# Cosine attention and a two-layer feed-forward on one core: from the third batch on, attention products in 64-row by 32-column tiles for two quads at once

## The chip, the cores and the metric

The kernel runs on one core of a Trainium2 chip. A core has a matrix engine (TensorE, "PE" in the profile, its weight loads "PEld"), a vector engine (VectorE, "DVE"), an activation engine (ScalarE, "ACT"), a general engine (GpSimd, "POOL") and a queue engine (SyncE, "SP"). The engines run their own instruction streams in order and wait for each other through semaphores. PE reads SBUF and writes PSUM, which has 8 banks of 128 partitions by 512 fp32; ACT and DVE read PSUM. The metric is the device time of one execution in microseconds; the median of three runs before the change is 428.21 us (426.97 to 428.27).

## The reference

Attention over 8 batches, 12 heads, 448 positions, 64 numbers per head, with queries and keys divided by their norms and the scores by tau = 0.1; then two matrix products with a leaky ReLU between:

```python
q_n = q / (norm(q) + 1e-06);  k_n = k / (norm(k) + 1e-06)
attn = softmax(q_n @ k_n.T / tau)          # per batch and head, 448 x 448
x = (attn @ v) as [8 * 448, 12 * 64]       # 3584 x 768
h = x @ w_in;  g = max(0.01 * h, h);  out = g @ w_out     # 768 -> 2048 -> 768
```

The scores are at most 10, so the kernel takes exp without subtracting the maximum.

## The kernel before, in words

A batch's 12 heads are 6 pairs, and 3 quads of two pairs (quad j has pairs 2j and 2j+1). A **slot** s is one pair of one batch, 0 to 47.

**Preparation of a slot.** Queries and keys are loaded (SP queue), squared on POOL (`squares`, L163), summed over each row on DVE (`sums`, L174), turned into norms by three small ACT instructions (`roots`, L181 to L183), inverted and multiplied in on DVE (`normalise`, L191 and L195), and transposed by a DMA on the SP queue (`transposes`, L227) into `qkT`, where PE reads them. `hold` (L426) is a one-element copy on POOL that makes POOL wait for the end of a slot's `normalise` before it squares the next slot.

**Attention.** A key tile is 128 keys of a pair's two heads against 448 queries: four products of 64 rows (one head's 64 numbers) by 64 columns (half of the keys), which write two PSUM banks (`key_tiles`, L251); ACT takes exp into a bf16 tile (L263). A quad has seven such tiles: three for each pair, and one that holds the last 64 keys of both pairs. `attend(j)` then makes three sets of products for the quad (L274): the sums of exp (weights are ones), and the values in two halves of the 64 numbers (e = 0, 1). Each set is 4 passes (3 main key tiles and the rest) of four 128-row by 32-column products, one head to a strip of 32 columns; in the pass for the rest, half of the 128 rows are weights of zero. ACT makes 1/sum by Ln and Exp (L285, L286) and DVE multiplies it into the values, writing `xT` (`scale`, L305).

**Feed-forward.** The 3584 rows are 8 chunks: of each two batches (896 rows) an even chunk of 384 rows that needs the first batch only, and an odd chunk of 512 that needs both. A chunk has 16 groups `first` (6 products of 128x128 by 384 or 512, then a leaky ReLU on ACT, L323 and L329) and 6 or 8 groups `second` (16 products by 384, then a copy of the result by DVE into `osb`, L359, and a store on the SP queue).

**Order.** There is no scheduler: instructions are issued in the order in which Python writes them. From the second batch on, attention goes in **units** (seven to a batch): in three of seven units an `attend`, then three key tiles, then `sums`, `roots` and `normalise` of a slot some units ahead with its transposes and loads, and then feed-forward groups of the batch before, as many as an even share allows. PSUM banks are dealt by `banks`, which takes the banks that were dealt longest ago. A unit with `attend` takes 9 banks (one for the sums, two for the values, six for the scores), one without takes six, before its feed-forward groups.

```python
            if at is not None:
                attend(b * NQ + at)
                load_v(b * NQ + at + 2)
            key_tiles([(b * NPAIR + p, ki) for p, ki in tiles])
            ...
            sums(s)
            roots(s)
            ...
                normalise(s)
            ...
            while len(queue) > 1 and (i == len(units) - 1 or done + queue[0][0] / 2 <= share):
                cost, fn = queue.pop(0)
                fn()
```

## Time and profile before

| | |
|---|---|
| Median of three runs | 428.21 us (426.97 to 428.27) |
| The profiled execution's own time | 427.37 us |
| Its span, first to last instruction | 425.6 us |
| PE busy | 414.2 us (97%) |
| ACT busy | 267.3 us (63%) |
| DVE busy | 187.8 us (44%) |
| POOL busy | 138.0 us (32%) |
| Mean granted PE clock | 0.998 |

The profile is of one execution. Busy time is the time in which at least one instruction of the engine is under way; PE's products are pipelined and overlap, so the start times in the timeline tell more of their pace than the durations. A line of the page or of the table of groups names the source line, the engine, the operation, what is written from what, the shape, the count, then busy time and mean duration. A line of the timeline gives a start, a duration and how many like instructions were merged.

### The profile page before, as it was taken

Reading aid. Unit: us, or ns where it says so; the run is one execution under the profiler, and the core shown is the slowest. Engines: PE = TensorE matmul, PEld = TensorE weight load, DVE = VectorE, ACT = ScalarE, POOL = GpSimd, SP = SyncE. Lnnn points to the kernel's source line nnn. Section 1 sums busy time; section 2 is a strip of 40 time slices with the busy share of each in tenths; the row PEclk is TensorE's granted clock in tenths of the full one; section 3 lists DMA queues with packets and bytes.
Section 4 is the critical chain, followed back from the end, with each engine's and each line's share of the span. In section 5 each row is a group of like instructions: output and inputs, shape, how many; then the busy total and the mean of one; then the engine's idle time right before and its main releaser. Section 6 shows DMA issues by size and latency. Waiting matters only on the chain.

```text
span 425.6 us, 9170 instructions
## 1 busy us (share of the span) xinstructions
PE 414.2 (97%) x3571; PEld 210.8 (50%) x3585; DVE 187.8 (44%) x367; ACT 267.3 (63%) x494; POOL 138.0 (32%) x208
## 2 busy tenths in 40 slices
PE   8789999999999999999999999999999999999995
PEld 3234555544555555544455555544455555554563
DVE  5886767443363445343453454553343541220021
ACT  3997886667644786577663786568745686434300
POOL 3876543523124233513224132621424110000000
PEclk9999999999999999999999999999999999999999
DMA  5999999965458555953758356864547322010022
GB/s 142 219 229 219 224 218 197 242 151 123 93 121 169 103 130 104 210 126 79 131 90 171 100 124 129 164 128 129 97 105 138 78 60 42 39 74 2 0 75 75
DMA packets 102890, 53.68 MB, mean 126 GB/s; under 512 B 68928, under 2 KB 97856, under 8 KB 102848
## 3 DMA queue, kind: packets, MB, share of 16 engines
q1 hardware_dynamic: 76880, 40.75, 40.0%
q0 software_dynamic: 25056, 11.80, 21.6%
q8 instruction: 28, 0.46, 0.5%
q10 hardware_dynamic: 912, 0.56, 0.4%
q14 instruction: 14, 0.11, 0.1%
HBM read 45.61 MB, written 11.01 MB: 133 GB/s over the span
## 4 chain that ended last, share of the span: by engine, by line
PE 82%; DMA 10%; ACT 4%; DVE 2%; issue 1%; POOL 1%; ACTq 0%; DVEq 0%; POOLq 0%; SPq 0%
PE ps L348 33%; PE ps L323 31%; PE ps L274 11%; PE ps L251 7%; DMA w_out_sb<-in_moe_w_out_dram 6%; DMA q_h<-in_q_dram 3%; ACT pe L263 2%; DVE qn L195 1%; DMA k_h<-in_k_dram 1%; POOL sq L163 0%; ACT pr L263 0%; ACT ss L183 0%; ACT ss L181 0%; ACT ss L182 0%; DVE ss L174 0%
## 5 line engine op out<-in xcount | busy, mean ns | idle before, releaser
L263 ACT ACTIVATE pe<-ps 128x896 bf16<-128x896 f32 x144 | 122.6, 918 | 47.9 <-PE ps L251 46.5
L348 PE MATMUL ps<-w_out_sb,hT 128*128 128x384 bf16 x896 | 152.0, 326 | 0.3 <-DMA w_out_sb<-in_moe_w_out_dram 0.3
L323 PE MATMUL ps<-xT,w_in_sb 128*128 128x384 bf16 (+1 forms) x757 | 150.2, 352 | 0.6
L348 PEld LDWEIGHTS <-hT 128*128 128x128 bf16 x896 | 85.2, 98 | 65.3 <-issue 10.0
L323 PEld LDWEIGHTS <-w_in_sb 128*128 128x128 bf16 x768 | 73.2, 98 | 73.1 <-issue 7.7
L329 ACT ACTIVATE hT<-ps 128x384 bf16<-128x384 f32 (+1 forms) x128 | 64.8, 540 | 41.1 <-PE ps L323 40.5
L426 POOL CAST seen<-qn 128x1 f32<-128x1 bf16 x47 | 8.6, 183 | 201.4 <-DVE qn L195 200.7
L359 DVE COPY osb<-ps 128x384 f32<-128x384 f32 (+1 forms) x56 | 30.9, 552 | 95.8 <-PE ps L348 89.4
L174 DVE TENSOR_REDUCE ss<-sq 128x6 f32<-128x384 f32 (+1 forms) x95 | 56.2, 612 | 19.8 <-POOL sq L163 18.2
L163 POOL TENSOR_TENSOR sq<-q_h 128x512 f32<-128x512 f32 x46 | 47.7, 1036 | 6.1 <-DMA q_h<-in_k_dram 5.0
L251 PE MATMUL ps<-qkT 64*64 64x448 bf16 (+1 forms) x636 | 44.7, 358 | 3.2 <-ACT pe L263 1.4
L191 DVE RECIPROCAL r<-ss 128x14 f32<-128x14 f32 x48 | 11.5, 241 | 78.5 <-ACT ss L183 78.5
L163 POOL TENSOR_TENSOR sq<-k_h 128x384 f32<-128x384 f32 x47 | 39.0, 830 | 6.0 <-DMA k_h<-in_k_dram 6.0
L305 DVE TENSOR_TENSOR xT<-ps,rb 128x448 bf16<-128x448 f32 x48 | 27.9, 619 | 29.6 <-ACT rb L286 28.1
L274 PE MATMUL ps<-pe,v_b 128*32 128x448 bf16 x576 | 35.6, 353 | 0.0
L195 DVE TENSOR_TENSOR qn<-q_h,r 128x512 bf16<-128x512 f32 x48 | 34.2, 713 | 2.2 <-DVE r L191 0.6
L285 ACT ACTIVATE rb<-ps 128x448 f32<-128x448 f32 x24 | 13.1, 544 | 32.8 <-PE ps L274 32.7
L251 PEld LDWEIGHTS <-qkT 64*64 64x64 bf16 (+1 forms) x636 | 14.8, 104 | 31.3 <-issue 23.8
L195 DVE TENSOR_TENSOR qn<-k_h,r 128x384 bf16<-128x384 f32 x48 | 27.1, 564 | 0.0
L263 ACT ACTIVATE pr<-ps 128x896 bf16<-128x896 f32 x24 | 22.2, 927 | 0.0
L274 PEld LDWEIGHTS <-v_b 128*32 128x32 bf16 x576 | 15.2, 97 | 11.9 <-issue 0.4
L150 POOL DMA_DIRECT2D v_rem<-in_v_dram x32 | 20.5, 646 | 0.0
(39 smaller groups left out, 183.1 us busy)
## 6 DMA issues: line engine op xcount, KB each, us to landing
q_h<-in_q_dram SPq DMA_DIRECT2D x48, 192.0 KB, 3.5
k_h<-in_k_dram SPq DMA_DIRECT2D x46, 192.0 KB, 3.7
out_dram<-osb SPq DMA_DIRECT2D x30, 192.0 KB, 3.1
v_b<-in_v_dram POOLq DMA_DIRECT2D x24, 192.0 KB, 5.2
out_dram<-osb SPq DMA_DIRECT2D x12, 384.0 KB, 3.1
w_in_sb<-in_moe_w_in_dram POOLq DMA_DIRECT2D x4, 768.0 KB, 10.5
w_out_sb<-in_moe_w_out_dram POOLq DMA_DIRECT2D x2, 1536.0 KB, 22.6
q_h<-in_q_dram SPq DMA_DIRECT2D x48, 32.0 KB, 3.7
```

The costliest lines, as they stand in the source:

```text
L150: gp.dma_start(out=vrb[b % 2][lo : lo + 64, :, g], in_=r[g])
L163: eng.tensor_tensor(sq, x, x, op=ALU.mult)
L174: nc.vector.tensor_reduce(o.rearrange("p (h t) -> p h t", h=2), sqs[s][i], axis=AX.X, op=ALU.add)
L195: nc.vector.tensor_tensor(qn[s][:, lo:hi], x.rearrange("p h t d -> p t h d"), r[:, r0 : r0 + 2 * nt].rearrange("p (h t) -> p t h", h=2) .u ...
L251: nc.tensor.matmul(out=sc[p : p + width, a, :S], lhsT=x[rows, c0 : c0 + width], rhs=x[rows, 0:S], start=True, stop=True,)
L263: nc.scalar.activation(out=dst, in_=sc[:, :, :S], func=AF.Exp, scale=inv_tau)
L274: nc.tensor.matmul(out=x[32 * g : 32 * g + 32, :S], lhsT=weights(g, ki) if ki < 3 else rem(g), rhs=pe[s][:, ki, a, :] if ki < 3 else pr[j] ...
L305: nc.vector.tensor_tensor(xT[m][:, 2 * jj + e, half * S : (half + 1) * S], pos.pop((j, e))[:, :S], rbs[j], op=ALU.mult,)
L323: nc.tensor.matmul(out=pm[:, :n], lhsT=w_in_sb[:, kt, m * 128 : (m + 1) * 128], rhs=xT[c // 2][:, kt, c0 : c0 + n], start=(kt == 0), stop= ...
L329: nc.scalar.activation(out=hT[c][:, m, :n], in_=pm[:, :n], func=AF.Prelu, alpha=0.01)
L348: nc.tensor.matmul(out=po2[:, :HALF], lhsT=hT[c][:, m, ts * 128 : (ts + 1) * 128], rhs=w_out_sb[:, m, half * HALF : (half + 1) * HALF], st ...
L359: nc.vector.tensor_copy(out=o[:, half * HALF : half * HALF + cut], in_=po2[:, :cut])
```

## The change

The first two batches (quads 0 to 5) stay as they are. For quads 6 to 23:

- **Key tiles.** A quad's seven tiles are each 64 keys of both of its pairs: eight products of 64 rows by 32 columns, four strips of 32 keys (two of one pair, two of the other) by two heads, into two banks as before (`quad_tiles`). All seven tiles are now full and alike. For this the keys are loaded in two halves (one more DMA per slot), and the values come as `vq`, in rows of 64 keys, by four DMAs per quad on POOL's queue (before: one per quad for the main keys and four per batch for the rest).
- **Sums and values.** They are made for a group of two quads at once (`group_products`): 7 passes of eight 64-row by 32-column products, into two banks, for the sums, for e = 0 and for e = 1. ACT's Ln and Exp become one pair of 128x896 per group; the multiplication into `xT` becomes four DVE instructions of 64 partitions by 448 per group and half. The last pass over zeros is gone.
- **Order.** The units become 42 **visits** of three tiles each, n = 0 to 41. A group's sums stand in the visit after its last tile, its two value halves in the two visits after that, each right behind that visit's three tiles. Then come `sums`, `roots`, `normalise`, the transposes and loads of one slot (visits 6, 13, 20, 27 and 34 have none, and there is none after visit 37), and then feed-forward groups. A chunk's groups are held back until the group with its last quad is done, and spread by a new rule. Three tiles and a set of products together take all 8 banks.
- **Pools.** One exp tile per key tile (27 buffers), 5 of `vq`, and one `hT` in place of two.

What the visits hold after their three tiles, in the order in which the program issues it:

| visit | products | feed-forward |
|---|---|---|
| 0 | | 1 second |
| 1 to 4 | | 4 first of 512, each |
| 5, 6, 7 | sums, e=0, e=1 | 1 second, each |
| 8, 9 | | 1 second, each |
| 10, 11, 12 | sums, e=0, e=1 | 1 second, each |
| 13 | | 8 first of 384 |
| 14 | sums | 8 first of 384 |
| 15, 16 | e=0, e=1 | 1 second, each |
| 17, 18 | | 2 second, each |
| 19, 20, 21 | sums, e=0, e=1 | 6, 4, 4 first of 512 |
| 22 | | 2 first, 1 second |
| 23 | | 2 second |
| 24, 25, 26 | sums, e=0, e=1 | 2, 1, 1 second |
| 27 | | 1 second, 3 first of 384 |
| 28, 29, 30 | sums, e=0, e=1 | 9 first, 4 first, 1 second |
| 31, 32 | | 2 second, each |
| 33 to 41 | sums 33, e=0 34, e=1 35; sums 38, e=0 39, e=1 40 | 31 groups in all |

After visit 41 come the last group's products and the rest of chunks 6 and 7.

```diff
-            engs[1].dma_start(out=k_h, in_=main(k, b, h0, 2))
+        if s < 2 * NEWQ:
+            engs[1].dma_start(out=k_h, in_=main(k, b, h0, 2))
+        else:
+            r = k[b, h0 : h0 + 2, 0:MAIN].rearrange("h (p u t) d -> u p h t d", u=2, t=3)
+            for u in range(2):
+                engs[1].dma_start(out=k_h[64 * u : 64 * u + 64], in_=r[u])
...
+    def quad_tiles(which):
+        tiles = []
+        for j, i in which:
+            sc = banks(2)
+            tiles.append(sc)
+            for strip in range(4):
+                x = qkT[2 * j + pair_in_half(j, strip // 2)]
+                c0 = 448 if i == 6 else 512 + 128 * (i % 3) + 64 * (i // 3)
+                c0 += 32 * (strip % 2)
+                for a in range(2):
+                    rows = slice(64 * a, 64 * a + 64)
+                    nc.tensor.matmul(
+                        out=sc[32 * strip : 32 * strip + 32, a, :S], lhsT=x[rows, c0 : c0 + 32],
+                        rhs=x[rows, 0:S], start=True, stop=True,
+                    )
+        for (j, i), sc in zip(which, tiles):
+            pq[j, i] = pe_tile()
+            nc.scalar.activation(out=pq[j, i], in_=sc[:, :, :S], func=AF.Exp, scale=inv_tau)
...
+    def group_products(g, e):
+        j0 = NEWQ + 2 * g
+        po = banks(2)
+        for i in range(7):
+            for strip in range(4):
+                for w in range(2):
...
+                    nc.tensor.matmul(
+                        out=po[32 * strip : 32 * strip + 32, w, :S],
+                        lhsT=weights, rhs=pq[j, i][rows, a, :],
+                        start=(i == 0), stop=(i == 6),
+                    )
+        if e is None:
+            rb = rbp.tile([128, 2, S], F32, name="rb")
+            nc.scalar.activation(rb, po[:, :, :S], func=AF.Ln)
+            nc.scalar.activation(rb, rb, func=AF.Exp, scale=-1.0)
...
+                nc.vector.tensor_tensor(
+                    xT[m][rows, 2 * jj + e, half * S : (half + 1) * S],
+                    po[rows, w, :S], grb[g][rows, w], op=ALU.mult,
+                )
...
+    for n, tiles in enumerate(visits):
+        if n == 0:
+            attend(NEWQ - 1)
+        quad_tiles(tiles)
+        if n in parts:
+            group_products(*parts[n])
...
+        s = b * NPAIR + 3 + u if u < 6 else NSLOT
+        sums(s)
+        roots(s)
+        if s < NSLOT:
+            normalise(s)
+            transposes(s)
+            load_qk(s + 4)
+            hold(qn[s][:, 6, 0, 0:1])
+            squares(s + 1)
+        for j, i in tiles:
+            if i == 0:
+                load_vq(j + 1)
+        done = 0
+        while held:
...
+            fn()
```

## The prediction

> **What bounds the kernel now.** First the page's busy shares and its slices, then the table by stretch:

> ```profile
> PE 414.2 (97%) x3571; PEld 210.8 (50%) x3585; DVE 187.8 (44%) x367; ACT 267.3 (63%) x494; POOL 138.0 (32%) x208
> PE   8789999999999999999999999999999999999995
> 105.00:387.00 282.00, 281.58 (x2492) 145.81 (x2497) 118.35 (x228) 180.51 (x330) 82.54 (x124) 1.00 0.54 112
> ```

> From 105 to 387 us PE is busy for 281.58 of 282 us at a granted clock of 1.00: nothing makes it wait. So each pass taken from PE is worth its price, and each wait put in costs its length. The timeline of PE gives the price of a pass:

> ```profile
> 200.87 0.75 PE L274 MATMUL ps<-pe,ones 128*32 128x448 bf16 x12
> 201.44 0.36 PE L274 MATMUL ps<-pr,ones_rem 128*32 128x448 bf16 x4
> 201.63 0.74 PE L274 MATMUL ps<-pe,v_b 128*32 128x448 bf16 x12
> ...
> 202.96 0.36 PE L274 MATMUL ps<-pr,v_rem 128*32 128x448 bf16 x4
> 203.25 0.76 PE L251 MATMUL ps<-qkT 64*64 64x448 bf16 x12
> 203.94 5.35 PE L323 MATMUL ps<-xT,w_in_sb 128*128 128x512 bf16 x23
> ```

> From 200.87 to 201.63 are 4 passes: 0.19 us each, four products at once. The last pass starts at 202.96, the next shape at 203.25 and not at 203.15: a change of tile shape costs 0.10. Three key tiles take 203.94 - 203.25 - 0.10 = 0.59, so 0.19 each.

> Then the timeline of all engines, where a slot is prepared as fast as it can be:

> ```profile
> 61.14 0.55 DVE L195 TENSOR_TENSOR qn<-k_h,r 128x384 bf16<-128x384 f32 x1
> 61.83 0.18 POOL L426 CAST seen<-qn 128x1 f32<-128x1 bf16 x1 [4.54 <-DVE qn L195]
> 62.03 1.03 POOL L163 TENSOR_TENSOR sq<-q_h 128x512 f32<-128x512 f32 x1
> 63.03 0.82 POOL L163 TENSOR_TENSOR sq<-k_h 128x384 f32<-128x384 f32 x1
> 63.09 1.34 DVE L174 TENSOR_REDUCE ss<-sq 128x8 f32<-128x512 f32 x2 [1.41 <-POOL sq L163]
> 64.47 0.31 ACT L181 ACTIVATE ss<-ss,tiny 128x14 f32<-128x14 f32 x1 [0.69 <-DVE ss L174]
> 65.05 0.31 ACT L183 ACTIVATE ss<-ss,eps 128x14 f32<-128x14 f32 x1
> 65.39 0.24 DVE L191 RECIPROCAL r<-ss 128x14 f32<-128x14 f32 x1
> 66.27 0.55 DVE L195 TENSOR_TENSOR qn<-k_h,r 128x384 bf16<-128x384 f32 x1
> ```

> One slot's `normalise` ends at 61.69, the next one's at 66.82. Every link waits for the one before: `hold` for `normalise`, squares for `hold`, sums for squares, `roots` for sums, `normalise` for `roots`. So 5.14 us is the shortest step from slot to slot, whatever PE does. A unit before lasts 8.2 us here (203.25 to the next tiles at 211.83), so that never showed. Last, where a copy of the feed-forward stands in DVE's order:

> ```profile
> 163.47 2.77 PE L348 MATMUL ps<-w_out_sb,hT 128*128 128x384 bf16 x16
> ...
> 167.44 0.55 DVE L195 TENSOR_TENSOR qn<-k_h,r 128x384 bf16<-128x384 f32 x1
> 167.91 0.55 DVE L359 COPY osb<-ps 128x384 f32<-128x384 f32 x1
> ```

> The group ends near 166.2, its copy starts at 167.91, behind the unit's `normalise`. Nobody needed the bank yet.

> **The change part by part.** The sum is made against the profiled execution's 427.37 us, 0.84 under the median.

> *Passes.* Key tiles stay at 126 for 18 quads. Sums and values fall from 18 x 12 = 216 to 9 x 21 = 189: 27 x 0.19 = 5.1 us less. The price of a pass of eight is shown nowhere. Bounds: 0.19, since row halves (the 64x64 tiles) and column strips (128x32) each already run side by side at 0.19; and 0.38, if the halves took turns. I take 0.19: the rows show both ways of splitting. [...]

> *Shape changes.* Scores and products now have one shape. Before: 42 units x 2, 18 more for the attends, 2 at the end: 104. After: 84 + 1 + 4 = 89. 15 x 0.10 = 1.5 us less. PE gains 6.6 in all.

> *Waits in short visits.* A second group is 16 x 0.1625 = 2.6 us (from 5.31 us between shape changes for 32 products, in the chain). A visit with one is 0.57 + 0.20 + 2.6 = 3.4 us of PE, with products (7 x 0.19) 4.7. Both are under 5.14, and in a visit with products all 8 banks are taken again, so the product pair takes the bank of the visit before's second group, whose copy stands behind `normalise`. Prices: exp 0.85 each from 0.43 after the tile's start (203.25 to 203.69); the three roots 0.87; sums 1.14; reciprocal and two products 1.41; copy 0.55; hand-over 0.06. The xT scaling is 4 x 0.58 = 2.3 (1.16 for two in the trace; a 64-partition form is not shown: between half, if all elements counted, and the same, as 448 per partition are unchanged; I take the same). Ln and Exp of 128x896: 544 and 576 ns at half the width; I take 0.85 and 0.95, as exp of 128x896 does.

> Visit 5 (sums): exps, Ln and Exp, roots, `normalise` end 7.46 us after its start, the copy 8.07. Visit 6's products could start at 4.86 + 0.67 = 5.53: **wait 2.54**. From visit 7's start as zero: products leave at 2.4, scaling 4.7, sums 5.85, roots 6.8, `normalise` of slot 21 at 8.2. Then:
> - Visit 9 opens quad 10, which needs slot 21 transposed: 8.2 + 2.95 (landing, the DMA part's 2.9, and hand-over) = 11.2; PE is there at 8.5: **2.75**.
> - Slots 22 and 23: 8.2 + 2 x 5.14 = 18.5. Copy 19.1. Visit 10's sums need its bank; PE is there at 15.0: **4.15**.
> - Slot 24, behind these sums and their Ln and Exp: 24.9 (6.3 later). Visit 11's products wait for the copy at 25.5; PE at 23.9: **1.62**.
> - Now a step is copy 0.61, products 1.57, scaling 2.3, sums 1.14, roots 0.99, `normalise` 1.41 = 8.0: slot 25 at 32.9. Visit 12: **3.34**. Slot 26 at 40.9, copy 41.5; visit 13's second first-group takes that bank: **2.27**.

> These make 16.7. The same order (an e = 0 visit with one second group, then e = 1) gives 3.34 at visits 16 and 26 each; visits 17 and 18, 31 and 32 with two second groups wait 0.64 + 1.77 each time for the copies of the visit before; visit 27 0.64, visit 30 1.86: 14.0 more. Visits 1 to 4, 14, 19 to 24, 28, 29 and 33 to 37 hold about 6 us of PE or more, visits 38 to 41 prepare nothing: some twenty waits under 0.6, 3.4 together, which I leave to the range. Sum 30.7.

> *Beside it.* ACT: 9 x 1.8 in place of 18 x 1.12, less in all, but in one lump ahead of `roots` (counted). POOL: 72 issues for values at 0.65 to 0.80 in place of 18 + 24: in a quad's first visit squares (2.2) and four issues (up to 3.2) make 5.4 against a step of 5.14, so up to 0.3 in the stretch of visits 7 to 9, in the range. SP: one more key DMA, 0.4 us: transposes 1.26, five loads 2.5 to 3, under 5.14. One `hT`: a chunk's last second group ends on PE before the next chunk's first, no price.

> 427.4 - 6.6 + 30.7 = 451.5, on the median's side **452 us**. [...]

> **The rivals.**
> - *Slack is lent (faster).* 33 preparations stand in some 260 us of PE: 8 us each against steps of 5 to 8, so short visits could live on what long ones leave. It speaks for it that slots are prepared two to three visits ahead, and that PE waits for almost nothing now. Against it: a bank can't be lent, as the next visit takes it. It decides where all waits stay under 6.6 us; with none, 428.2 - 6.6 = 421.6.
> - *Waits only where a bank is forced.* Visits 6, 12, 16, 26 and part of 10, without what they hand on: 10 to 17 us, 432 to 438.
> - *The clock drops in the waits.* Granted 1.00 throughout, but no PE wait over 1.5 us stands in this trace. If each of the four waits of 3.3 us and more halved the clock for as long again, 4 x 1.7 = 7 us: 459. [...]
> - *Row halves take turns.* 315 x 0.19 = 60 us more: 487 without waits, 512 with them.

> **How the numbers follow.** Waits as worked out, with or without the clock (440 to 464): 0.61. Forced waits only (428 to 440): 0.17. Slack lent (419 to 426.9): 0.17. No difference beyond 0.3%, 1.3 us, about what a measurement can tell (426.9 to 429.5): 0.03. Over 464: 0.02. The range 428 to 464 leaves out the faster cases and the top: 0.8 inside. Faster 0.17, same 0.03, slower 0.80.

> **What would show it.** Right: PE waits on DVE's osb copy at the product line's first products in visits 6, 10, 11, 12, 16 and 26, 2 to 4 us each; on qkT's transposes once, in visit 9; DVE's sums wait on POOL's squares in step; passes of eight at 0.19. Wrong: PE still 97% busy, or passes at 0.38, or `normalise` well under 5 us after the last one's, or copies issued before it.

## The result and the profile after

The changed kernel takes 460.07 us (median of six runs, 458.07 to 461.37), the kernel before beside it 428.03 us: 1.075 times as long, with a 95% interval of 1.0719 to 1.0781. Forecast were 452 us, 428 to 464. The profiled execution took 461.37 us, 34.0 more than the profiled one of before; the sum of the prediction had 24.1.

The busy time of PE, its slices and the granted clock, from the page of the changed kernel:

```profile
PE 423.1 (92%) x4720; PEld 216.9 (47%) x4737; DVE 214.2 (47%) x403; ACT 265.7 (58%) x476; POOL 152.7 (33%) x238
PE   8789999999878699699999879998999999999996
PEclk9999999999897989989999989999999999999999
```

PE was a full row of nines. Now the slices from the eleventh on have holes, and the clock has them nearly where PE has. The table by stretch, from the same start to 34 us later than 387, as the profiled execution is 34 us longer:

```profile
105.00:421.00 316.00, 291.64 (x3618) 152.71 (x3613) 142.25 (x259) 177.10 (x309) 93.45 (x147) 0.97 0.48 99
```

PE is idle for 24.4 of 316 us, where it was idle for 0.4 of 282, and its clock is 0.97. What PE waited for (line waited for: us in all, times, longest), in the view of waits:

```profile
PE ps L378 <- DVE osb L449: 15.5, 6, 3.5
PE ps L438 <- DVE osb L449: 3.5, 3, 1.6
PE ps L355 <- DMA qkT<-qn: 2.5, 1, 2.5
```

L378 is the products of `group_products`, L438 the `second` groups, L355 the tiles of `quad_tiles`, L449 the copy of a `second` group out of its bank. The timeline shows one such wait, in visit 6 (lines of PE and DVE; those of the other engines are left out):

```profile
115.35 0.76 PE L355 MATMUL ps<-qkT 64*32 64x448 bf16 x24
...
116.19 0.24 DVE L216 RECIPROCAL r<-ss 128x14 f32<-128x14 f32 x1 [3.60 <-ACT ss L208]
116.47 0.69 DVE L220 TENSOR_TENSOR qn<-q_h,r 128x512 bf16<-128x512 f32 x1
117.07 0.55 DVE L220 TENSOR_TENSOR qn<-k_h,r 128x384 bf16<-128x384 f32 x1
117.54 0.55 DVE L449 COPY osb<-ps 128x384 f32<-128x384 f32 x1
...
118.15 1.67 PE L378 MATMUL ps<-pe,vq 64*32 64x448 bf16 x56 [2.04 <-DVE osb L449]
...
119.75 4.25 PE L438 MATMUL ps<-w_out_sb,hT 128*128 128x384 bf16 x16
```

The group whose bank is copied had ended by 115.35. DVE sat idle for 3.60 us until `roots` (L208) came, then did `normalise` first and the copy after it. The first products waited 2.04 us for that bank. The `second` group behind them, 2.77 us elsewhere, took 4.25: the granted clock was 0.50 from 119.38 to 122.79 (shown under the hardware below). This is called the half clock from here on.

The step from slot to slot, on DVE, a few visits later:

```profile
137.00 0.55 DVE L220 TENSOR_TENSOR qn<-k_h,r 128x384 bf16<-128x384 f32 x1
137.47 0.55 DVE L449 COPY osb<-ps 128x384 f32<-128x384 f32 x1
138.96 1.34 DVE L199 TENSOR_REDUCE ss<-sq 128x8 f32<-128x512 f32 x2 [0.94 <-POOL sq L188]
141.26 0.24 DVE L216 RECIPROCAL r<-ss 128x14 f32<-128x14 f32 x1 [0.96 <-ACT ss L208]
...
142.15 0.55 DVE L220 TENSOR_TENSOR qn<-k_h,r 128x384 bf16<-128x384 f32 x1
```

From one `normalise` to the next are 5.15 us (forecast 5.14), and between them DVE waits for POOL's squares and then for ACT's roots. The price of a pass of eight can be read in visit 8, in PE's timeline:

```profile
128.88 0.76 PE L355 MATMUL ps<-qkT 64*32 64x448 bf16 x24
129.57 2.77 PE L438 MATMUL ps<-w_out_sb,hT 128*128 128x384 bf16 x16
```

Three tiles and a change of shape take 129.57 - 128.88 = 0.69 us: 0.19 or 0.20 a pass, when 0.10 is taken off for the change.

### The profile page after: what moved, and what is told of

It is laid out like the page before. It is cut to its first block, busy times and chain, and to the rows that moved or that the text cites. A ratio compares the mean times of both kernels' runs of the same rounds, so it can differ in the third digit from the quotient of the medians.

```text
span 459.5 us, 11553 instructions
## 1 busy us (share of the span) xinstructions
PE 423.1 (92%) x4720; PEld 216.9 (47%) x4737; DVE 214.2 (47%) x403; ACT 265.7 (58%) x476; POOL 152.7 (33%) x238
## 4 chain that ended last, share of the span: by engine, by line
PE 60%; DMA 14%; DVE 12%; ACT 6%; issue 4%; SPq 1%; POOL 1%; DVEq 0%; POOLq 0%
PE ps L413 25%; PE ps L438 22%; PE ps L378 9%; DMA w_out_sb<-in_moe_w_out_dram 5%; DVE xT L397 5%; DMA q_h<-in_q_dram 4%; PE ps L355 4%; DMA q_h<-in_k_dram 3%; DVE ss L199 3%; DVE qn L220 3%; DVE osb L449 1%; ACT ss L208 1%; POOL sq L188 1%; ACT ss L206 1%; ACT pe L361 1%
## 5 line engine op out<-in xcount | busy, mean ns | idle before, releaser
L438 PE MATMUL ps<-w_out_sb,hT 128*128 128x384 bf16 x896 | 158.4, 335 | 4.8 <-DVE osb L449 3.5
L361 ACT ACTIVATE pe<-ps 128x896 bf16<-128x896 f32 x126 | 106.3, 921 | 32.1 <-PE ps L355 31.9
L438 PEld LDWEIGHTS <-hT 128*128 128x128 bf16 x896 | 87.4, 100 | 76.3 <-issue 22.6
L397 DVE TENSOR_TENSOR xT<-ps,rb 64x448 bf16<-64x448 f32 x72 | 44.8, 622 | 64.1 <-PE ps L378 63.3
L449 DVE COPY osb<-ps 128x384 f32<-128x384 f32 (+1 forms) x56 | 30.7, 552 | 69.8 <-PE ps L438 69.2
L206 ACT ACTIVATE ss<-ss,tiny 128x14 f32<-128x14 f32 x48 | 14.8, 309 | 56.0 <-DVE ss L199 55.4
L378 PE MATMUL ps<-pe,vq 64*32 64x448 bf16 x1008 | 30.3, 368 | 13.4 <-DVE osb L449 13.3
L288 ACT ACTIVATE pe<-ps 128x896 bf16<-128x896 f32 x42 | 35.8, 916 | 5.9 <-PE ps L279 4.5
L355 PE MATMUL ps<-qkT 64*32 64x448 bf16 x1008 | 33.4, 353 | 3.2 <-DMA qkT<-qn 2.5
L378 PEld LDWEIGHTS <-vq 64*32 64x32 bf16 x1008 | 16.5, 95 | 24.8 <-issue 15.4
L169 POOL DMA_DIRECT2D vq<-in_v_dram x36 | 23.0, 638 | 0.5 <-issue 0.3
L173 POOL DMA_DIRECT2D vq<-in_v_dram x36 | 22.5, 624 | 0.0
```

The source lines that it names most:

```text
L288: nc.scalar.activation(out=dst, in_=sc[:, :, :S], func=AF.Exp, scale=inv_tau)
L355: nc.tensor.matmul(out=sc[32 * strip : 32 * strip + 32, a, :S], lhsT=x[rows, c0 : c0 + 32], rhs=x[rows, 0:S], start=True, stop=True,)
L361: nc.scalar.activation(out=pq[j, i], in_=sc[:, :, :S], func=AF.Exp, scale=inv_tau)
L378: nc.tensor.matmul(out=po[32 * strip : 32 * strip + 32, w, :S], lhsT=weights, rhs=pq[j, i][rows, a, :], start=(i == 0), stop=(i == 6),)
L397: nc.vector.tensor_tensor(xT[m][rows, 2 * jj + e, half * S : (half + 1) * S], po[rows, w, :S], grb[g][rows, w], op=ALU.mult,)
L438: nc.tensor.matmul(out=po2[:, :HALF], lhsT=hT[c][:, m, ts * 128 : (ts + 1) * 128], rhs=w_out_sb[:, m, half * HALF : (half + 1) * HALF], st ...
```

## The experiments

The theory: the added time is PE's waits for banks and transposes, because short visits run into the chain of preparing a slot, and because a bank's copy stands behind `normalise`. The rivals: passes of eight are dearer than 0.19; the half clock alone costs the time; what bounds is the chain's length, not the place of the copy. Ratios are to the kernel before, on the same chip.

| kernel | median us | ratio, 95% interval |
|---|---|---|
| changed kernel | 460.07 | 1.0750 (1.0719 to 1.0781) |
| narrow_tiles | 428.05 | 1.0006 (0.9993 to 1.0019) |
| filled_waits | 458.51 | 1.0719 (1.0685 to 1.0754) |
| no_hold | 466.67 | 1.0909 (1.0875 to 1.0944) |
| squares_ahead | 458.15 | 1.0714 (1.0676 to 1.0751) |
| remainders_by_pool | 460.93 | 1.0777 (1.0742 to 1.0811) |
| late_normalise | 443.00 | 1.0364 (1.0336 to 1.0392) |
| late_squares_ahead | 440.47 | 1.0288 (1.0255 to 1.0321) |
| three_moves | 435.54 | 1.0177 (1.0139 to 1.0214) |
| three_moves_gap | 432.59 | 1.0095 (1.0062 to 1.0128) |
| four_moves | 426.73 | 0.9972 (0.9961 to 0.9983) |

### The price of a pass of eight: narrow_tiles

The kernel before, with its key tiles in 64x32 products from the third batch on: eight products a pass in place of four, and nothing else.

```diff
     for b in range(1, B):
+        if b == 2:
+            deals["width"] = 32
```

> The kernel before with one change: from the third batch on its key tiles are eight products of 64 rows by 32 columns in place of four of 64 by 64; order, sums and values are as before. If a pass of eight costs 0.19 us, as a pass of four, the time is that of before within 0.3%. [...]

No difference. Its timeline of PE, where the prediction's rows of before had twelve products for three tiles:

```profile
204.18 0.76 PE L251 MATMUL ps<-qkT 64*32 64x448 bf16 x24
204.87 5.35 PE L323 MATMUL ps<-xT,w_in_sb 128*128 128x512 bf16 x23
```

Twice as many products, and the same 0.69 us to the next shape. Row halves and column strips run side by side: in turn, 126 passes would have taken 126 x 0.19 = 24 us more. In the trace of the changed kernel, in visit 8, the eight products of a pass start 2 to 5 ns apart and the next pass some 0.17 us later, and the 24 of the visit start within 0.41 us (128.875 to 129.287).

### The place of the copy: late_normalise

`normalise`, transposes, loads, `hold` and squares are issued behind the visit's first feed-forward group instead of ahead of it. `sums` and `roots` stay where they were.

```diff
-        if s < NSLOT:
-            normalise(s)
-            transposes(s)
-            load_qk(s + 4)
-            hold(qn[s][:, 6, 0, 0:1])
-            squares(s + 1)
...
             fn()
             done += w
+            if not prepared:
+                prepare(s, tiles)
+                prepared = True
```

> The changed kernel with one move: normalise, the transposes, the loads and the squares of a visit stand behind its first feed-forward group, so the copy of that group's result comes ahead of normalise in DVE's order. If the waits come from copies queued behind normalise, the products of visits 6, 10 and 11 wait for nothing, those of 12, 16 and 26 for 1 to 1.5 us, the clock drops once at most, and the time falls by 20 to 27 us, to 433 to 440. If the preparation chain itself is too slow for short visits (5.14 us and more from slot to slot), the waits only change their names and the time stays within 455 to 462.

443.0 us: 17 of the 32 us are gone by a change of order alone, 3 us less than the least that was expected. The stretch of visit 6 again, DVE and PE of this kernel:

```profile
115.08 0.76 PE L355 MATMUL ps<-qkT 64*32 64x448 bf16 x24
115.26 0.56 DVE L449 COPY osb<-ps 128x384 f32<-128x384 f32 x1 [2.94 <-PE ps L438]
115.87 1.52 PE L378 MATMUL ps<-pe,vq 64*32 64x448 bf16 x56
115.92 0.24 DVE L216 RECIPROCAL r<-ss 128x14 f32<-128x14 f32 x1
```

The copy now goes as soon as its group ends, and the products start 0.79 us after the tiles, where it was 2.80. The waits of this kernel:

```profile
PE ps L355 <- DMA qkT<-qn: 6.0, 3, 2.7
PE ps L378 <- DVE osb L449: 4.2, 5, 1.4
```

Waits for the copy at L378 fall from 15.5 to 4.2. What the expectation didn't have: in their place slots 21 and 23 come later, 2.5 and 2.7 us of wait for transposes, and the mean granted clock of the profiled execution is 0.990, where the changed kernel has 0.975 and the kernel before 0.998.

### The half clock alone: filled_waits

Seven of PE's waits (visits 6, 9, 10, 11, 12, 16 and 26) are filled with 3 to 14 products of constants, 128x128 by 512, into a bank that the real products behind them overwrite. This adds work and takes away none.

```diff
+    def busy(x, count):
+        for i in range(count):
+            nc.tensor.matmul(out=x, lhsT=warm[:, :128], rhs=warm, start=True, stop=True)
...
+        busy(po[:, FILLED[g, e][0], :], FILLED[g, e][1]) if (g, e) in FILLED else None
```

> The changed kernel with idle products (128x128 by 512, into a bank that nobody reads) ahead of the seven waits of over 1 us in visits 6, 9, 10, 11, 12, 16 and 26, a little shorter than the wait each. If the half clock after these waits costs what its six stretches of 3.4 us make (six times 1.7), the granted clock is 1.00 throughout and the time falls by 8 to 10 us, to 450 to 452, with the start of each waiting product set where it was. If the clock does not matter, or the waits are lengthened by what was put in, the time stays within 2 us of 460.

In the profiled execution the clock holds: the table by stretch has 1.00 where the changed kernel had 0.90.

```profile
130.00:200.00 70.00, 62.72 (x815) 32.97 (x819) 35.76 (x66) 40.46 (x73) 27.44 (x43) 1.00 0.59 113
```

But the median falls by 1.6 us only, which the two intervals can't tell from none, and the profiled time by 4.9 (456.47 against 461.37). The expectation of 8 to 10 is missed. Visits 6, 9, 12, 16 and 26 are 1.5 to 1.7 us shorter each, as half a half-clock stretch should give (3.41 / 2 = 1.7); visits 11, 13, 17 and 18 are 0.4 to 1.5 longer. The one that grew most, visit 13, in PE's timeline:

```profile
160.91 1.15 PE L424 MATMUL ps<-xT,w_in_sb 128*128 128x384 bf16 x6
164.38 6.99 PE L424 MATMUL ps<-xT,w_in_sb 128*128 128x384 bf16 x42 [2.33 <-DVE osb L460]
```

In the changed kernel visit 13 waits 1.01 us in all, here 2.33 at this one place. A PE that gets ahead of DVE meets the next bank that isn't free. More than half of the half clock's price was time that PE would have waited anyway.

### A link taken out of the chain: no_hold, squares_ahead

`hold` keeps POOL from squaring a slot before the slot before it is normalised. no_hold leaves it out from visit 0 on; squares_ahead keeps it and squares slot s + 2 in place of s + 1 behind it (with one set of squares ahead of visit 0).

```diff
-            hold(qn[s][:, 6, 0, 0:1])
...
-            squares(s + 1)
+            squares(s + 2)
```

The first line is no_hold, the others squares_ahead.

> The changed kernel without hold from visit 0 on, so that POOL squares a slot as soon as its loads have landed and POOL is free; nothing else moves. If the waits come from copies queued behind normalise, only the stretch of visits 8 to 11 gains, where a step was the bare 5.14 us, and the time falls by 2 to 6 us; the waits of visits 6, 16 and 26 stay at 2 to 3.7 us. If the chain from slot to slot is the cause by itself, the waits fall by half or more, with 12 us or more off the time.

> The changed kernel with POOL squaring the slot after the next one behind hold, where it squared the next one: the sums of a slot no longer wait for squares that wait for the last normalise, and the squares still start right after a normalise, not in the middle of one. If the loss without hold (6.6 us) came from squares running beside DVE's multiplications, this one gains 2 to 6 us on the changed kernel (454 to 458) and the multiplications keep 0.69 and 0.55 us; if it came from the order of loads and transposes on the SP queue, it stays over 460.

no_hold was 6.6 us slower than the changed kernel, against both readings of its expectation. The groups of DVE and POOL (mean ns of one is the number after the busy time), of no_hold:

```profile
L188 POOL TENSOR_TENSOR sq<-k_h 128x384 f32<-128x384 f32 x47 | 43.3, 921 | 5.6 <-DMA k_h<-in_k_dram 5.6
L220 DVE TENSOR_TENSOR qn<-k_h,r 128x384 bf16<-128x384 f32 x48 | 33.9, 707 | 0.0
```

and of the changed kernel:

```profile
L188 POOL TENSOR_TENSOR sq<-k_h 128x384 f32<-128x384 f32 x47 | 39.1, 831 | 5.6 <-DMA k_h<-in_k_dram 5.6
L220 DVE TENSOR_TENSOR qn<-k_h,r 128x384 bf16<-128x384 f32 x48 | 27.1, 564 | 0.0
```

Without `hold` POOL squares a slot while DVE normalises another, and both slow down. At its worst:

```profile
140.64 1.26 POOL L188 TENSOR_TENSOR sq<-k_h 128x384 f32<-128x384 f32 x1
141.14 1.17 DVE L220 TENSOR_TENSOR qn<-k_h,r 128x384 bf16<-128x384 f32 x1
```

0.83 became 1.26 and 0.55 became 1.17. So `hold` is a link of the chain and earns its place. That the overlap makes up all of the 6.6 us isn't shown: this kernel also waited 4.1 us for one slot's transposes, and the `second` group behind that took 4.83 us (from 137.66) in place of 2.77; the mean granted clock of its profiled execution is 0.968, of the changed kernel's 0.975. squares_ahead, which takes squares out of the chain without the overlap (0.69 and 0.55 us for the multiplications in three_moves, which is built on it: 135.02 and 135.63), gains 1.9 us on the changed kernel, too little to tell from none, and between its two expectations. A likely reason, not tested by itself: with the copies still behind `normalise`, the chain runs through `sums` and `roots` at the product visits, and squares were not the last link there.

### What is left: late_squares_ahead, three_moves, three_moves_gap

Both moves together; then `sums` and `roots` issued ahead of the products as well (so the roots don't wait behind the group's Ln and Exp on ACT, nor the sums behind the scaling on DVE); then slots 21, 27, 33, 39 and 45 prepared one visit earlier.

```diff
         quad_tiles(tiles)
+        b, u = 2 + n // 7, n % 7
+        s = b * NPAIR + 3 + u if u < 6 else NSLOT
+        sums(s)
+        roots(s)
         if n in parts:
             group_products(*parts[n])
```

```diff
-        s = b * NPAIR + 3 + u if u < 6 else NSLOT
+        s = NSLOT if n and u == 0 else b * NPAIR + 3 + u
```

> The two moves together: normalise behind the first feed-forward group, and squares two slots ahead. If copies behind normalise and the chain from slot to slot are two links of one path, the gains add: 443 less 3 to 9 us, 434 to 440. If the copies were all of it, 442 to 444.

> Both moves, and the sums and roots of a slot ahead of the visit's products, so that DVE adds up before it scales and ACT makes roots before Ln and Exp. If preparation and the two kinds of copies out of PSUM in DVE's and ACT's order are the whole loss, nearly all waits are gone (one for slot 21's transposes in visit 9 stays, 1 to 2 us), and the 6.6 us off PE show: 425 to 430. If PE's short visits cost by themselves, it stays over 434.

> The same, and slot 21 (and 27, 33, 39, 45) prepared in the visit before, 6, 13, 20, 27 and 34, which prepared nothing; 7, 14, 21, 28 and 35 prepare nothing instead. The wait for slot 21 in visit 9 goes: 1 to 2 us less than with three moves, 423 to 429.

440.5, 435.5 and 432.6 us. All three missed their expectations, by 0.5, 5.5 and 3.6 us. three_moves also lies over the 434 that was to speak for short visits as a cost by themselves; its waits say otherwise. In three_moves the large waits for copies are gone, and what stays are two for transposes, 7.2 us in all. Behind the second, of 5.23 us, passes of products start 0.37 to 0.38 us apart (their weight loads at 145.19, 145.57 and 145.94), twice the 0.19; the mean granted clock is 0.986. In three_moves_gap one of 2.99 us is left. That wait, in lines of SP, DVE and PE of three_moves_gap:

```profile
132.99 0.53 SPq L126 DMA_DIRECT2D q_h<-in_q_dram  x1
133.61 1.38 SPq L132 DMA_DIRECT2D k_h<-in_k_dram  x2
...
134.41 0.55 DVE L220 TENSOR_TENSOR qn<-k_h,r 128x384 bf16<-128x384 f32 x1
...
135.04 1.53 SPq L134 DMA_DIRECT2D q_h<-in_q_dram  x1
136.63 0.61 SPq L134 DMA_DIRECT2D q_h<-in_k_dram  x1
137.35 1.26 SPq L252 DMA_TRANSPOSE qkT<-qn  x1
...
141.34 0.57 PE L355 MATMUL ps<-qkT 64*32 64x448 bf16 x8 [2.99 <-DMA qkT<-qn]
```

Slot 23 is normalised at 134.97, but SP is issuing five loads of another slot until 137.24. Its transposes are issued 2.4 us late.

### SP's queue: four_moves, remainders_by_pool

The two 32 KB loads of the remaining keys and queries (L134) go to POOL's queue, behind the squares: in four_moves on top of the three moves and the earlier slots, in remainders_by_pool on the changed kernel alone.

```diff
-            load_qk(s + 4)
+            load_qk(s + 4, later=True)
             hold(qn[s][:, 6, 0, 0:1])
             squares(s + 2)
+            load_rem(s + 4, (gp, gp))
```

(remainders_by_pool has `squares(s + 1)` here.)

> The three moves with the earlier slots, and each slot's two 32 KB remainder loads issued by POOL behind the squares instead of by SP behind the transposes. In three_moves_gap PE's one large wait (2.99 us at 138.35, for slot 23's transposes) stands where SP was still issuing slot 26's five loads: normalised at 134.97, the transposes were issued at 137.35 and reached PE 3.99 us later. Theory (SP's queue holds that transpose): SP's loads end at about 134.9, the transposes are issued at 135.05 and land at 139.0; the wait is 0.7 us, the half clock behind it is gone, visit 11 falls from 9.53 to about 5.6 us, and the time from 432.6 to 428.6 us (427.5 to 430.5), level with the kernel before. Rival (the transfer itself is late, by traffic on the DMA engines): the transposes take longer to land by as much as they are issued earlier, and the time stays at 431 to 434 us.

> The changed kernel with that one move alone (the two remainder loads issued by POOL behind the squares). In the changed kernel SP issues the transposes of the slots that PE waits for within 0.1 us of their normalise (137.55 to 137.61), so SP's queue should be no cause there. Theory: no change beyond 2 us either way, 458 to 462 us. Rival (SP's five loads are the added work that makes the slots late): 450 us or less.

four_moves takes 426.73 us (ten runs, 426.53 to 427.92), a little under the kernel before: 0.28% faster, with an interval that lies wholly below 1. The same wait in its timeline:

```profile
134.09 0.55 DVE L227 TENSOR_TENSOR qn<-k_h,r 128x384 bf16<-128x384 f32 x1
...
134.76 2.21 SPq L259 DMA_TRANSPOSE qkT<-qn  x1
...
138.68 0.38 PE L362 MATMUL ps<-qkT 64*32 64x448 bf16 x8 [0.65 <-DMA qkT<-qn]
```

The transposes are issued 0.1 us after `normalise` and reach PE 3.92 us later, against 3.99 before. So it was the queue and not the transfer; the wait is 0.65 (expected 0.7), and no half clock follows (1.00 in the table by stretch below). The time came out 1.9 us under the expectation and 0.8 under its range. A wait for slot 29's transposes in visit 18 went too (the visit took 6.66 us in three_moves_gap, 6.00 here), which is a third of that; the rest is open. remainders_by_pool stayed at 460.93, as expected: in the changed kernel SP's queue is not what holds the slots. The queue became the next limit when that was gone.

four_moves' busy time of PE, and its stretch of the prediction's table:

```profile
PE 413.0 (97%) x4737; PEld 213.7 (50%) x4737; DVE 210.0 (49%) x403; ACT 266.1 (62%) x476; POOL 185.9 (44%) x296
```

```profile
105.00:387.00 282.00, 280.23 (x3625) 149.26 (x3610) 137.37 (x258) 177.37 (x309) 121.52 (x197) 1.00 0.57 110
```

## Why the prediction was right, and where it was short

The chain, the banks and the visits that wait were forecast as they came, and the time lies in the range; the sum fell 8 us short of it. From the first tile of visit 0 to the last product's start the profiled executions took 338.55 us before and 371.97 after; the difference, 33.4, and 0.6 ahead of it make the 34.0. Each visit's length less the price of its instructions gives its wait, and where its clock was half, 1.7 us of each stretch of 3.41 is set apart.

| term | forecast | measured |
|---|---|---|
| passes and shape changes | -6.6 | -6.6 (not measured: the same prices) |
| waits of the visits named | 30.7 | 26.7 |
| small waits, left to the range | 0 (3.4) | 3.1 (what is left over) |
| half clock, left to a rival | 0 (7) | 10.2 |
| sum | 24.1 | 33.4 |

**Passes and shapes, -6.6: the passes right, the shape changes not seen.** The price of 0.19 was tested by itself (narrow_tiles). four_moves needs only 0.5 us less than before over the same part (338.0), with 6.1 us left over by the same prices. Of these 2.9 are waits in visits 7, 11, 13, 17 and 27. Nearly all of the rest, some 3 us, comes in bits of 0.10 to 0.24 in each of the other 22 visits with products, where the products follow the tiles: visit 5 of the changed kernel takes 2.20 us from its first tile to its `second` group (110.44 to 112.64), where 0.57 + 1.33 + 0.10 = 2.00 was priced. The prediction gave this step no price, because the shape stays the same. Whether PE itself needs the time or waits for something is open. Either way it takes back more than the 1.5 us that fewer changes of shape were to save, and about 3.5 of the 6.6 us can be seen.

**The scaling of `xT`, "the same" by 64 partitions as by 128: right.** L397 takes 622 ns on average, its form of 128 partitions (L305 of before) took 619. Four together take 2.53 us, forecast 2.3.

**Waits: the mechanism right, single sizes off.** Forecast and measured: visit 6 2.54 and 2.18, visit 9 2.75 and 2.96, visit 11 1.62 and 1.22, visit 12 3.34 and 3.55, visits 16 and 26 3.34 each and 3.62 and 3.41, visit 30 1.86 and 1.85. Too large were visit 10 (4.15, measured 2.29), visit 13 (2.27, measured 1.01) and visit 17 (0.64, measured 0.03). The copies and qkT stood as what is waited for in the visits that the prediction named, as the waits view has it. The place of the cause was tested: moving `normalise` behind the group alone gave back 17 us.

**The half clock and the small waits: what the sum left out.** The sum, 24.1, is 9.3 us short of the 33.4. It had no term for the half clock; the rival gave 7 us, on the author's estimate that four waits of 3.3 us and more would halve the clock for as long again. That a wait halves the clock, no run showed then: the trace of before has the half clock once, behind the last product (PE ends at 421.0, the clock is 0.50 from 424.00 to 425.60), so it was not 1.00 throughout. In the changed kernel it came six times among the products, also behind the waits of visits 6, 9 and 10, which are 2.0 to 2.5 us long, and the account above sets 10.2 us apart for it. But waits and half clock are not two costs that add. In filled_waits, with a full clock, the visits' waits come to 35.6 us by the same account, against 30.7 in the sum and 34.1 with the small waits; in the changed kernel they come to 29.8 and the half clock to 10.2. So of the 9.3 us 4.9 stay without any half clock: 1.8 in the visits named and 3.1 in small amounts, which the sum put at nothing. The other 4.4 went with it in the profiled executions, 1.6 in the medians. That the small amounts come near the 3.4 left to the range is luck: they were to be waits for copies, and most of them are the step from tiles to products. With a full clock visits 10, 13 and 17 wait 4.0, 2.5 and 0.9 us, near the 4.15, 2.27 and 0.64 that were forecast: in the changed kernel they came out smaller because PE at half clock came later to a bank that was late anyway.

**Slips in the working.** A unit before lasts 211.83 - 203.25 = 8.58 us, not 8.2. Visit 5's chain to the end of `normalise` was put at 7.46 us; the prices listed for its links add up to 7.12 with one hand-over, and it took 7.18. Row halves in turn come to 421.6 + 60 = 482 us without waits, not 487; the 512 with waits is right. None of them changes what was forecast.

**The rivals.** Row halves in turn: fallen, by narrow_tiles. Waits only where a bank is forced, 432 to 438: fallen, since visits 9, 11, 13, 18, 30 and 32 waited too. The clock drops in the waits, 459: nearest by its number, 1 us off, but in part by luck: six stretches in place of four, whose removal gave back less than their length. Slack lent: fallen for this order of instructions, but with four moves of order 426.73 us was reached, so little stood between this change and a small gain. SP, which the prediction passed with "under 5.14", was no cause in the changed kernel, but became one as soon as two slots came 3.5 us apart (432.59 to 426.73 us by moving two of its loads).

## What to carry to other kernels

When a change makes stretches of work on the bounding engine shorter, look at what was hidden behind their old length: here a chain of 5.15 us over POOL, DVE, ACT and back, which 8 us of PE had covered and 3.4 to 4.9 didn't. A copy that frees a PSUM bank belongs ahead of work that waits for something else on the same engine; this order cost more than the whole edit could save, and one move of it was worth 17 us. When the first limit goes, the next queue shows (SP's loads ahead of a transpose), so a repair is judged by the new trace, not by the sum of the waits it takes away.

## What the runs showed of the hardware

**The half clock behind idle stretches of PE.** All six stretches among the products of the changed kernel last 3.413 us and start at 119.38, 136.45, 143.28, 160.34, 194.48 and 266.16: 5, 2, 5, 10 and 21 times 3.413 apart. The table by stretch for the first of them and for the 3.41 us ahead of it (length, then PE's busy time; the granted clock is the third number from the end):

```profile
115.97:119.38 3.41, 1.37 (x64) 0.79 (x55) 1.87 (x4) 2.60 (x4) 1.60 (x3) 1.00 0.36 56
119.38:122.79 3.41, 3.41 (x26) 1.49 (x11) 2.49 (x4) 0.00 (x0) 0.41 (x1) 0.50 0.66 154
```

and for two stretches of this length in remainders_by_pool:

```profile
117.08:120.49 3.41, 1.40 (x56) 0.79 (x55) 1.87 (x4) 2.44 (x4) 1.86 (x3) 1.00 0.46 67
120.49:123.91 3.42, 3.42 (x48) 1.83 (x41) 2.98 (x5) 0.21 (x1) 1.33 (x3) 1.00 0.93 147
```

**POOL and DVE side by side.** Squares of 384 fp32 on POOL and a product of 384 fp32 by a broadcast on DVE took up to 1.26 and 1.17 us where they ran at the same time (no_hold, 140.64 and 141.14), 0.82 and 0.55 where they did not (changed kernel, 138.89 and 142.15).
